# Two chunks of the attention in float32 corners of the array

## The chip, the cores and the metric

The kernel runs on one core of one Trainium2 chip. The metric is the time of one execution on the device in microseconds (us). In the names of the profile, PE is TensorE (matrix products), PEld its weight loads, DVE VectorE, ACT ScalarE, POOL GpSimd and SP SyncE, which issues all DMA transfers here. A program that fixes one order of the instructions on each engine stands behind both kernels; the engines wait for each other by semaphores.

## The reference

A linear attention with a decaying state feeds a feed-forward layer (FFN) with a maximum over three branches.

```python
batch, n_heads, seq, head_dim = (4, 8, 768, 48)
...
for t in range(S):
    kt, vt, rt = (k[:, :, t], v[:, :, t], r[:, :, t])
    cur = np.einsum('bhd,bhe->bhde', u[None] * kt, vt)
    y[:, :, t] = np.einsum('bhd,bhde->bhe', rt, state + cur)
    state = w[None, :, :, None] * state + np.einsum('bhd,bhe->bhde', kt, vt)
...
h = np.maximum(np.maximum(x @ w1, x @ w2), x @ w3)     # x: 3072 x 384, w1 to w3: 384 x 768
return (h @ w_out).astype(np.float32)                  # w_out: 768 x 384, weights in float64
```

## The kernel before

The sequence is cut into 12 chunks of 64 steps (C = 64). A chunk has two halves q of 4 heads, and a half is 8 units (2 pairs of heads by 4 batches). A unit holds two heads: one in partitions 0 to 63, the other in 64 to 127. For each half the attention needs these products, all of them on PE into tiles of the PSUM pool `psa` (4 buffers), and these are the words used below:

- **scores** (sc): the decayed keys kT against the decayed r, 64 by 64 for each head; masked on DVE (`mask`) into the tile am.
- **bonus** (bo): the diagonal of am, from the product pp = kT * rT (`joined`) and a fixed operand spots; DVE lays it on the diagonal (`on_diagonal`).
- **keys turned** (th): the keys transposed against an identity; needed for the state.
- **keys** (ke): the turned keys against v, which are added to the state (`into_state`).
- **values** (va): v against am and the state against r; ACT and DVE take them out as x in two float16 parts, xh and xl (`x_high`, `x_low`).

The FFN of a chunk multiplies x (256 columns, the 64 steps of 4 batches) by 18 weight blocks of three products of three terms each (`up`, hi*hi + hi*lo + lo*hi in float16), takes maxima and multiplies by the third matrix (`down`); these products go into `psm` (4 buffers).

Chunks 1 to 11 work in float16 parts as well: ACT makes the high part of kT, r, am, v, the turned keys and the state, DVE the low part, and a pair of DMAs (`spread`) lays both into a block-diagonal tile, in which the two heads of a unit are one 128 by 128 operand: kd into kb (scores, keys turned), ktd into ktb (keys), vd into vb and sd into sb (values). Chunk 0 is computed in float32: ACT lays kT into the blocks kb and kbx, v into vb and the turned keys into ktb and ktbx (`apart`), and `full` multiplies by operands of 128, 96 or 112 columns. Chunks 0 to 2 (c < EARLY) take their bonus from pp; from chunk 3 on POOL scales k and r and computes the bonus.

The weights come as 16 halves of blocks (words of float64, 576 KB each) into 4 buffers `raw64`; each half takes an ACT cast (`tops`), a DVE `convert`, an ACT `round_up` and a DVE `leave` to become two float16 parts (w_97 to w_104, the last two for `down`). The buffer is free when `leave` is done.

The order of all this is worked out before the program is written: every step is announced with a due time, an engine and a cost (`plan.do`), the table SHIFT adds a correction to the due time for each kind and stage of the program, and `Plan.order` runs a list of ready steps by due time. At the start `stir` runs 20 products of zeros on PE.

## Time and profile before

| | |
|---|---|
| median of 3 runs | 407.06 us (404.7 to 408.22) |
| the profiled execution | 404.66 us |
| its span, first to last instruction | 402.9 us |
| PE busy | 382.0 us (95% of the span) |
| DVE, ACT, POOL busy | 286.8, 264.2, 185.3 us |
| mean granted clock of TensorE | 0.973 of full speed |

The profiled execution is one run with the profiler on; what lies between its span and its time (1.76 us) is start and end outside the core's instructions. Busy times overlap across engines. The granted clock is one number for a stretch of time: 1.00 is 2.4 GHz, 0.50 is 1.2 GHz.

### The profile page before, as it was taken

To read this page: it belongs to the slowest core of one execution; us is meant where nothing else is said; L and a number is where in the kernel's file an instruction comes from. 1 tells how busy PE (TensorE), PEld (TensorE's weight loads), DVE (VectorE), ACT (ScalarE), POOL (GpSimd) and SP (SyncE) were. 2 spreads that over 40 slices of the span, in tenths; PEclk is the share of its full clock that TensorE was granted. 3 is DMA by queue.
4 is the path that set the end of the run, shared out by engine and by line. 5 is a ranking of instruction groups with operands and counts; after the bars stand their busy time and mean duration, and the time that the engine had idled before them with its cause. 6 is when DMAs were issued, how large, how long until landed. Compare 5 with 4: busy or idle time off the path is not lost.

```text
span 402.9 us, 12298 instructions
## 1 busy us (share of the span) xinstructions
PE 382.0 (95%) x4898; PEld 342.4 (85%) x4898; DVE 286.8 (71%) x540; ACT 264.2 (66%) x699; POOL 185.3 (46%) x188
## 2 busy tenths in 40 slices
PE   8699979989999899999999999999999999999994
PEld 4599869879898788999999989988898998999883
DVE  6675999975988978826957948948858875634520
ACT  6865978676776676554764854865775976984421
POOL 9330110184698766415475466465576463120110
PEclk9856999999999999999999999999999999999999
DMA  7877899999969997838678678698599686820101
GB/s 237 306 239 214 247 259 291 250 243 265 253 186 255 248 257 206 211 93 242 188 224 245 181 201 255 173 275 236 136 286 265 160 250 178 219 65 2 39 2 48
DMA packets 29809, 81.89 MB, mean 203 GB/s; under 512 B 4656, under 2 KB 10288, under 8 KB 29744
## 3 DMA queue, kind: packets, MB, share of 16 engines
q1 hardware_dynamic: 29744, 81.03, 72.9%
q8 instruction: 40, 0.66, 0.7%
q14 instruction: 25, 0.20, 0.2%
HBM read 37.59 MB, written 4.72 MB: 105 GB/s over the span
## 4 chain that ended last, share of the span: by engine, by line
PE 63%; DMA 15%; DVE 7%; ACT 6%; issue 5%; SPq 2%; POOL 2%; DVEq 0%; ACTq 0%; POOLq 0%
PE psm L660 48%; PE psa L573 10%; DMA kb<-kd 6%; DMA raw<-in_wo_dram 3%; DMA ktb<-ktd 3%; PE psa L655 2%; DMA tok<-in_tok_dram 2%; PE psa L557 2%; DVE m L679 1%; DMA u_sb<-in_ut_dram 1%; ACT junk L481 1%; POOL feat L499 1%; ACT xh L638 1%; DVE xl L643 1%; DVE sd L628 1%
## 5 line engine op out<-in xcount | busy, mean ns | idle before, releaser
L660 PEld LDWEIGHTS <-w 128*128 128x128 f16 x2592 | 249.3, 98 | 33.3 <-issue 5.0
L660 PE MATMUL psm<-xh,w 128*128 128x256 f16 x1296 | 222.0, 273 | 3.0 <-DVE m L679 1.6
L660 PE MATMUL psm<-xl,w 128*128 128x256 f16 x648 | 153.3, 273 | 0.3 <-DVE xl L643 0.2
L679 DVE SCALAR_TENSOR_TENSOR m<-psm,m 128x256 f32<-128x256 f32 x144 | 60.1, 419 | 38.7 <-PE psm L660 23.0
L688 POOL TENSOR_TENSOR hl<-m,hh 128x256 f16<-128x256 f32 x55 | 39.3, 720 | 89.5 <-ACT hh L682 89.5
L660 PE MATMUL psm<-hh,w 128*128 128x256 f16 x432 | 56.1, 272 | 0.0
L682 ACT CAST hh<-m 128x256 f16<-128x256 f32 x72 | 28.1, 401 | 40.5 <-DVE m L679 40.0
L499 POOL TENSOR_TENSOR feat<-feat,wrt 128x512 f32<-128x512 f32 x36 | 48.3, 1353 | 10.1 <-DMA feat<-in_feat_dram 9.0
L481 ACT ACTIVATE junk<-tok 128x384 bf16<-128x384 f32 x72 | 37.4, 519 | 15.5 <-DMA tok<-in_tok_dram 14.5
L643 DVE SCALAR_TENSOR_TENSOR xl<-psa,xh 32x256 f16<-32x256 f32 (+2 forms) x60 | 28.3, 471 | 13.8 <-ACT xh L638 12.8
L534 POOL TENSOR_TENSOR pp<-feat 128x512 f32<-128x512 f32 x4 | 7.6, 1911 | 57.5 <-DVE feat L499 47.9
L675 ACT ACTIVATE m<-psm 128x256 f32<-128x256 f32 x72 | 27.0, 375 | 10.5 <-PE psm L660 6.7
L660 PE MATMUL psm<-hl,w 128*128 128x256 f16 x216 | 33.4, 273 | 0.0
L573 PE MATMUL psa<-ah,vb 128*128 128x64 f16 x352 | 32.9, 193 | 0.0
L573 PE MATMUL psa<-rh,sb 128*128 128x64 f16 x352 | 32.5, 193 | 0.4 <-DMA sb<-sd 0.2
L573 PE MATMUL psa<-al,vb 128*128 128x64 f16 x176 | 31.2, 193 | 0.7 <-DVE al L593 0.7
L573 PE MATMUL psa<-rl,sb 128*128 128x64 f16 x176 | 31.2, 193 | 0.0
L573 PEld LDWEIGHTS <-vb 128*128 128x128 f16 x528 | 29.0, 98 | 1.7 <-issue 0.9
L628 DVE SCALAR_TENSOR_TENSOR sd<-state,wc,sd 128x192 f16<-128x192 f32 x44 | 29.5, 710 | 0.0
L518 POOL TENSOR_TENSOR am<-tok,u_sb 128x384 f32<-128x384 f32 x18 | 19.8, 1099 | 20.8 <-DVE al L593 15.9
L573 PEld LDWEIGHTS <-sb 128*128 128x128 f16 x528 | 27.5, 98 | 0.6 <-DMA sb<-sd 0.3
L638 ACT ACTIVATE xh<-psa 32x256 f16<-32x256 f32 (+2 forms) x60 | 24.9, 415 | 4.6 <-PE psa L573 3.0
(116 smaller groups left out, 609.6 us busy)
## 6 DMA issues: line engine op xcount, KB each, us to landing
tok<-in_tok_dram SPq DMA_DIRECT2D x24, 576.0 KB, 6.7
feat<-in_feat_dram SPq DMA_DIRECT2D x22, 512.0 KB, 4.5
raw<-in_ws_dram SPq DMA_DIRECT2D x12, 576.0 KB, 6.1
kb<-kd SPq DMA_DIRECT2D x22, 256.0 KB, 5.2
kb<-kd SPq DMA_DIRECT2D x22, 248.0 KB, 5.8
ktb<-ktd SPq DMA_DIRECT2D x20, 256.0 KB, 5.3
ktb<-ktd SPq DMA_DIRECT2D x20, 248.0 KB, 5.5
out_dram<-io SPq DMA_DIRECT2D x36, 128.0 KB, 2.6
```

The costliest lines, as they stand in the source:

```text
L481: nc.scalar.activation(out=junk[:, 0:U * D].rearrange("p (u d) -> p u d", u=U), in_=src, func=AF.Square, scale=scale, accum_out=stat[:, ki ...
L499: helper(c).tensor_tensor(out=t[n], in0=t[n], in1=tb, op=ALU.mult)
L518: helper(c).tensor_tensor(out=w.rearrange("p (g b) d -> p g b d", g=2), in0=t["r"], in1=by_token(u_sb, q), op=ALU.mult)
L573: nc.tensor.matmul(out=ps, lhsT=l[i], rhs=rr[j], start=first and n == 0, stop=last and n == 2)
L628: nc.vector.scalar_tensor_tensor(out=sd[q].dense[:, 1, us, 0:D], in0=state[:, j], scalar=wc[:, j:j + 1], in1=sd[q].dense[:, 0, us, 0:D], o ...
L638: nc.scalar.mul(out=hi, in_=src, mul=SC_X)
L643: nc.vector.scalar_tensor_tensor(out=lo, in0=src, scalar=SC_X, in1=hi, op0=ALU.mult, op1=ALU.subtract)
L660: nc.tensor.matmul(out=ps, lhsT=a, rhs=b, start=first and n == 0, stop=last and n == len(prods) - 1)
L675: nc.scalar.mul(out=m, in_=ps, mul=by)
L679: nc.vector.scalar_tensor_tensor(out=m, in0=ps, scalar=by, in1=m, op0=ALU.mult, op1=ALU.max)
L682: nc.scalar.copy(out=h[0][:, f, :], in_=m)
L688: lows_by(c, f).tensor_tensor(out=h[1][:, f, :], in0=m, in1=h[0][:, f, :], op=ALU.subtract)
```

## The change

Chunk 1 is computed in float32 too (FULL = 2), and both chunks in another form. Scores, keys turned and keys take kT, rT, the turned keys (a plain tile kt) and v as they lie in memory, without block-diagonal operands: each head of a unit is one product of 64 by 64 (48 columns for the keys), whose operands lie in partitions 0 to 63 or 64 to 127 and whose result goes to the same partitions of PSUM (`corners`). 16 such products replace 8 of 128 columns in chunk 0, and 24, 16 and 24 float16 products in chunk 1. Only the values still need block-diagonal operands: v is loaded by DMA straight into its places in vb (`load_values`, pieces of 48 floats), and for chunk 1 POOL lays the decayed state into sb (`state_apart`). With this go, for chunk 1, the float16 parts of kT, r, am, v and the turned keys and the spreads into kb, ktb and vb, and for the state after chunk 0 its parts and the spread into sb; for chunk 0 the `apart` copies on ACT.

POOL instead of DVE now scales kT and rT of chunks 1 and 2. The clearing of kb moves from DVE and shrinks. `stir` is announced six more times with two products of 512 columns each, due last (FILLS). A path that would compute xl by products (`x_taken_off`) is there, but with APART = 0 no chunk takes it; its two tiles minus and moved are filled all the same, on POOL. The clock model of the planner and the whole table SHIFT are new, so the order of steps changes on every engine through the whole program. Chunks 2 to 11 and the FFN keep their arithmetic.

```diff
-EARLY = 3
+FULL, EARLY, APART = 2, 3, 0
+FILLS = 6
...
-    STAGES = (1.6, 4.2)
+    RATE = {"feat": 330e3, "tok": 330e3, "word": 330e3, "again": 330e3, "u": 330e3, "vl": 200e3, "kb": 215e3, "ktb": 240e3, "sb": 240e3, "vb": 220e3, "io": 300e3}
+    STAGES = (-0.01, 1.6, 4.2)
...
-        "act ah": (9.25, -3.6, 2.69),
-        "act hh": (-13.49, -31.97, -10.54),
...
+        "act ah": (3.099, -10.12, -11.987, -18.156),
+        "act hh": (33.605, 41.616, -9.662, 26.229),
...
+    def load_values(c, q, hh):
+        w = vb[q].wide[HS[hh], :, hh * D:(hh + 1) * D].rearrange("p (g b) d -> p g b d", g=2)
+        nc.sync.dma_start(out=w, in_=tok[c, q][HS[hh], 2])
...
-    kb = Block("kb", P, nc.vector)
-    kbx = Block("kbx", P)
+    vb = [Block(f"vb{q}", 2 * D) for q in range(2)]
     amt = [const.tile([P, U, C], F32, name=f"am{q}") for q in range(2)]
-    nc.gpsimd.memset(amt[0], 0.0)
-    vb = [Block("vb0", 2 * D)]
-    nc.gpsimd.memset(amt[1], 0.0)
-    vb.append(Block("vb1", 2 * D))
+    for t in amt:
+        nc.gpsimd.memset(t, 0.0)
     for z in ztop:
         nc.gpsimd.memset(z.bitcast(F32), 0.0)
-    ktb = Block("ktb", P)
-    ktbx = Block("ktbx", P)
+    if FULL > 1:
+        sb = [Block(f"sb{q}", 2 * D) for q in range(2)]
+    moved = const.tile([P, 2, NJ, P], F16, name="moved")
+    nc.gpsimd.memset(moved.bitcast(F32), 0.0)
     kd = Block("kd", P)
+    kb = Block("kb", P, edge=C)
     vd = [Block(f"vd{q}", 2 * D) for q in range(2)]
+    ktd = Block("ktd", P)
+    ktb = Block("ktb", P, edge=C)
...
-        helper(c).tensor_tensor(out=t[n], in0=t[n], in1=tb, op=ALU.mult)
+        (nc.gpsimd if c else nc.vector).tensor_tensor(out=t[n], in0=t[n], in1=tb, op=ALU.mult)
...
+    def corners(ps, n, l, r):
+        for i in range(U):
+            for hh in range(2):
+                nc.tensor.matmul(out=ps[HS[hh], i, 0:n], lhsT=l(i, hh), rhs=r(i, hh), start=True, stop=True)
+
     def keys_turned(c, q):
         t = raws[c, q]
-        if c == 0:
-            t["th"] = psa.tile([P, U, D], F32, name="psa")
-            for i in range(U):
-                nc.tensor.matmul(out=t["th"][:, i, :], lhsT=(kb, kbx)[q].wide[:, i, :], rhs=eye[:, 0:D], start=True, stop=True)
+        if c < FULL:
+            t["th"] = psa.tile([P, U, C], F32, name="psa")
+            k = units(t["kT"])
+            corners(t["th"], C, lambda i, hh: k[HS[hh], i, :], lambda i, hh: eye[HS[hh]])
...
+            t["kt"] = work.tile([P, U, C], F32, name="kt")
+            nc.scalar.copy(out=t["kt"], in_=t.pop("th"))
+            return
...
+            k, r = units(t["kT"]), units(t["rT"])
+            corners(t["sc"], C, lambda i, hh: k[HS[hh], i, :], lambda i, hh: r[HS[hh], i, :])
...
+            corners(t["ke"], D, lambda i, hh: t["kt"][HS[hh], i, :], lambda i, hh: vb[q].wide[HS[hh], i, hh * D:(hh + 1) * D])
...
+        joint = c < APART
+        for i in range(U):
+            if c < FULL:
+                n = R
+                prods = [(vb[q].wide[:, i, 0:R], t["a"][:, i, :])]
+                if c:
+                    prods.append((sb[q].wide[:, i, 0:R], units(t["rT"])[:, i, :]))
...
+    def state_apart(q):
+        for hh in range(2):
+            w = sb[q].wide[HS[hh], :, hh * D:(hh + 1) * D].rearrange("p (g b) d -> p g b d", g=2)
+            by = wc[HS[hh], 2 * q:2 * q + 2].unsqueeze(2).unsqueeze(3).broadcast_to([C, 2, B, D])
+            nc.gpsimd.tensor_tensor(out=w, in0=state[HS[hh], 2 * q:2 * q + 2], in1=by, op=ALU.mult)
...
+    def values_fetched(c, q, due):
+        for hh in range(2):
+            dma(due + 0.01 * hh, lambda hh=hh: load_values(c, q, hh), 98304, writes=[("vb", q), ("vl", q)], kind="vl")
...
+    def entire(c, q, due):
+        f, v = ("feat", c, q), ("vb", q)
+        k, r, last = ("kT", c, q), ("rT", c, q), c + 1 == FULL
         scaled(c, q, due)
-        do(due - 0.29, "act", 1.05, lambda: apart((kb, kbx)[q], units(raws[c, q]["kT"]), C), reads=[("kT", c, q)], writes=[b], kind="kba")
-        do(due - 0.10, "act", 0.85, lambda: apart(vb[q], units(raws[c, q]["v"]), D, SC_V), reads=[t], writes=[("vb", q)], kind="vba")
+        do(due, "pe", 1.3, lambda: scores(c, q), reads=[f, k, r], takes=[("psa", ("sc", c, q))], active=0.66, kind="sca")
         before_mask(c, q, due)
-        do(due, "pe", 1.75, lambda: full("sc", q, (kb, kbx)[q], C, P, units(raws[c, q]["rT"])), reads=[f, b, ("rT", c, q)], takes=[("psa", ("sc", c, q))], active=0.5, kind="sca")
         do(due + 0.02, "dve", dve(U * C), lambda: mask(c, q), reads=[("sc", c, q)], writes=[("am", c, q)])
-
-    def first_values(q, due):
-        c = 0
-        do(due, "pe", 1.32, lambda: full("va", q, vb[q], C, R, raws[c, q]["a"]), reads=[("am", c, q), ("vb", q)], takes=[("psa", ("va", c, q))], active=0.66, kind="vaa")
-        leave_x(c, q, due)
-
-    def first_keys(q, due):
-        c, t, b, k = 0, ("tok", 0, q), ("kb", "kbx")[q], ("ktb", "ktbx")[q]
-        do(due - 0.30, "pe", 1.75, lambda: keys_turned(c, q), reads=[b], takes=[("psa", ("th", c, q))], active=0.4, kind="tha")
-        do(due - 0.24, "act", 0.85, lambda: apart((ktb, ktbx)[q], raws[c, q].pop("th"), C), reads=[("th", c, q)], writes=[k], kind="ktba")
-        do(due, "pe", 1.55, lambda: full("ke", q, (ktb, ktbx)[q], D, C + D, units(raws[c, q]["v"])), reads=[k, t], takes=[("psa", ("ke", c, q))], active=0.43, kind="kea")
-        after_keys(c, q, due)
+        do(due + 0.1, "pe", 1.29 * (2 if c else 1), lambda: values(c, q), reads=[("am", c, q), v] + ([f, r, ("sb", q)] if c else []), takes=[("psa", ("va", c, q))], active=0.66, kind="vaa")
+        leave_x(c, q, due + 0.1)
+        do(due + 0.2, "pe", 1.3, lambda: keys_turned(c, q), reads=[f, k], takes=[("psa", ("th", c, q))], active=0.66, kind="tha")
+        do(due + 0.22, "act", act(U * C), lambda: keys_laid(c, q, 0), reads=[("th", c, q)], takes=[("kt", ("kt", c, q))])
+        do(due + 0.3, "pe", 1.2, lambda: keys(c, q), reads=[("kt", c, q), v], takes=[("psa", ("ke", c, q))], active=0.55, kind="kea")
+        after_keys(c, q, due + 0.3)
...
+        if c + 1 < FULL:
+            do(due + 0.06, "pool", 2.0, lambda: state_apart(q), reads=[s], writes=[("sb", q)], near=0.55)
+            return
...
+    for k in range(FILLS):
+        do(90, "pe", 0.43, lambda: stir(2, 2 * TOK), reads=["stirred"] if k else [], writes=["stirred"], takes=[("psm", ("fill", k))], kind="fill")
+    attend(0, -0.8)
```

The names in the orders that follow: psa and psm are the PSUM pools; feat holds kT and rT, cs the identity, tok the values and vb, am, spots and pp are as above. First PE, from the end of the 20 stir products to the first float16 product, before:

```order
L412 MATMUL psa<-cs,tkf 128x128 x4
L655 MATMUL psa<-feat,kb 128x64 x8
L544 MATMUL psa<-pp,spots 128x256 x2
L655 MATMUL psa<-feat,kbx 128x64 x8
L544 MATMUL psa<-pp,spots 128x256 x2
L655 MATMUL psa<-am_161,vb_164 96x64 x8
L557 MATMUL psa<-cs,kb 128x48 x8
L655 MATMUL psa<-am_162,vb_167 96x64 x8
L544 MATMUL psa<-pp,spots 128x256 x2
L655 MATMUL psa<-tok,ktb 112x48 x8
L557 MATMUL psa<-cs,kbx 128x48 x8
```

Each batch of 8 here is one half's product, in operands of 96 to 128 columns. The same place on PE now, to the second values product:

```order
L573 MATMUL psa<-cs,feat 64x64 x16
L573 MATMUL psa<-feat 64x64 x16
L562 MATMUL psa<-pp,spots 128x256 x2
L573 MATMUL psa<-vb_160,kt 64x48 x16
L562 MATMUL psa<-pp,spots 128x256 x2
L662 MATMUL psa<-am_164,vb_160 96x64 x8
L573 MATMUL psa<-cs,feat 64x64 x16
L573 MATMUL psa<-feat 64x64 x16
L429 MATMUL psa<-cs,tkf 128x128 x4
L573 MATMUL psa<-vb_162,kt 64x48 x16
L662 MATMUL psa<-am_165,vb_162 96x64 x8
```

Scores, keys turned and keys have become batches of 16 corners, and the keys now stand here for both halves. From there to the FFN's first products:

```order
L382 LDWEIGHTS still
L382 MATMUL psm<-still 128x512
L382 LDWEIGHTS still
L382 MATMUL psm<-still 128x512
L573 MATMUL psa<-cs,feat 64x64 x16
L573 MATMUL psa<-feat 64x64 x16
L562 MATMUL psa<-pp,spots 128x256 x2
L573 MATMUL psa<-vb_160,kt 64x48 x16
L716 LDWEIGHTS w_97
```

Chunk 0 has its keys ahead of its values, all float32 work of chunk 0 stands ahead of the FFN, and so do keys turned, scores, bonus and keys of chunk 1's first half. After these follow 18 FFN products, the values of chunk 1's first half, the bonus and scores of its second half, 45 FFN products, its values, and the rest of chunk 1 between FFN products. Before, the keys of the second half of chunk 0 and all of chunk 1 but keys turned and scores of one half stood behind the FFN's first product.

SP, which issues the transfers in this order, from the load of chunk 1's first half on, before (L281 loads kT and rT, L292 v, L330 weights, L442 and L443 spread):

```order
L281 DMA feat<-in_feat_dram 128x1024
L292 DMA tok<-in_tok_dram 128x384
L281 DMA feat<-in_feat_dram 128x1024
L330 DMA raw_286<-in_ws_dram 128x2304
L330 DMA raw_303<-in_ws_dram 128x2304
L442 DMA kb<-kd 64x2048
L443 DMA kb<-kd 64x1984
L330 DMA raw_345<-in_ws_dram 128x2304
L330 DMA raw_362<-in_ws_dram 128x2304
L292 DMA tok<-in_tok_dram 128x384
L281 DMA feat<-in_feat_dram 128x1024
L442 DMA vb_164<-vd_177 64x1536
```

Between the weights stand a spread into kb and one into vb. The same now (L287 and L298 are these loads, L340 weights):

```order
L287 DMA feat<-in_feat_dram 128x1024
L298 DMA vb_160<-in_tok_dram 64x8x48 x2
L340 DMA raw_356<-in_ws_dram 128x2304
L287 DMA feat<-in_feat_dram 128x1024
L340 DMA raw_404<-in_ws_dram 128x2304
L298 DMA vb_162<-in_tok_dram 64x8x48 x2
L340 DMA raw_436<-in_ws_dram 128x2304
L340 DMA raw_492<-in_ws_dram 128x2304
L340 DMA raw_546<-in_ws_dram 128x2304
L287 DMA feat<-in_feat_dram 128x1024
L302 DMA tok<-in_tok_dram 128x384
L340 DMA raw_577<-in_ws_dram 128x2304
```

The spreads of chunk 1 are gone from between the weights; loads of v in pieces stand there instead.

POOL, after it has cleared the tiles, now (before, the first of these places held four pp products and nothing else until chunk 3's scaling):

```order
L418 ISA
L418 TENSOR_SCALAR minus<-cs 128x128
L420 TENSOR_SCALAR moved<-cs 32x32 x3
L418 TENSOR_SCALAR minus<-cs 128x128
L420 TENSOR_SCALAR moved<-cs 32x32 x3
L668 TENSOR_TENSOR sb_170<-state,wc 64x8x48 x2
L517 TENSOR_TENSOR feat<-feat,wrt 128x512 x2
L552 TENSOR_TENSOR pp<-feat 128x512
L668 TENSOR_TENSOR sb_172<-state,wc 64x8x48 x2
```

The scaling of chunk 1 now stands on POOL behind the unused minus and moved and behind the first half's state.

## Rows read from the trace of the kernel before

**Rows 1.** The page: the span, and the granted clock in 40 slices of it.

```profile
span 402.9 us, 12298 instructions
...
PEclk9856999999999999999999999999999999999999
```

**Rows 2.** Windows: stretch, length, busy of PE, PEld, DVE, ACT, POOL, PEclk, DMA share, GB/s.

```profile
9.00:12.80 3.80, 3.80 (x31) 3.56 (x30) 0.48 (x1) 3.67 (x9) 3.80 (x6) 1.00 1.03 421
12.80:15.60 2.80, 0.01 (x1) 0.03 (x1) 1.78 (x4) 2.77 (x5) 0.91 (x2) 1.00 1.00 401
...
16.00:16.50 0.50, 0.50 (x3) 0.40 (x2) 0.50 (x2) 0.50 (x1) 0.00 (x0) 0.62 0.06 22
...
20.00:34.00 14.00, 14.00 (x69) 13.61 (x69) 10.21 (x17) 9.09 (x18) 3.54 (x1) 0.50 0.74 231
34.00:36.40 2.40, 2.40 (x45) 2.34 (x45) 0.00 (x0) 0.48 (x1) 0.00 (x0) 0.50 1.00 270
...
36.60:38.00 1.40, 1.40 (x14) 1.26 (x13) 1.40 (x3) 0.43 (x2) 0.00 (x0) 1.00 0.87 273
36.20:396.80 360.60, 350.06 (x4714) 315.91 (x4711) 263.47 (x494) 239.38 (x652) 168.60 (x164) 1.00 0.74 201
40.00:80.00 40.00, 36.71 (x490) 32.55 (x488) 39.61 (x77) 32.46 (x73) 4.11 (x3) 1.00 0.99 261
```

**Rows 3.** Chain that ended last, 10 to 40 us: start, length, what.

```profile
17.52 2.79 PE psa L655 x16
20.32 3.39 PE psa L557 x16
23.70 2.59 PE psa L655 x16
```

**Rows 4.** Timeline of PE, 7 to 47 us: start, length, what, idle before.

```profile
7.78 0.60 PE L412 MATMUL psa<-cs,tkf 128*128 128x128 f32 x4
8.21 1.94 PE L655 MATMUL psa<-feat,kb 128*128 128x64 f32 x16
9.99 1.08 PE L544 MATMUL psa<-pp,spots 128*128 128x256 f32 x4
10.91 1.90 PE L655 MATMUL psa<-feat,kbx 128*128 128x64 f32 x16
15.61 1.55 PE L544 MATMUL psa<-pp,spots 128*128 128x256 f32 x4 [2.80 <-DVE pp L534]
...
36.20 0.40 PE L660 MATMUL psm<-xh,w 128*128 128x256 f16 x1
...
45.23 1.68 PE L655 MATMUL psa<-tok,ktbx 128*112 128x48 f32 x16
46.75 0.27 PE L660 MATMUL psm<-xh,w 128*128 128x256 f16 x1
```

**Rows 5.** Chain that ended last, 84 to 122 us: float16 products of a half.

```profile
90.50 0.40 PE psa L562 x16
90.89 0.70 PE psa L573 x24
95.53 1.41 PE psa L573 x48
...
117.39 0.60 PE psa L573 x24
```

**Rows 6.** Groups by line and shape on DVE, 0 to 80 us: busy, mean ns.

```profile
L499 DVE TENSOR_TENSOR feat<-feat,wrt 128x512 f32<-128x512 f32 x12 | 7.9, 683 | 0.3 <-DMA feat<-in_feat_dram 0.3
...
L628 DVE SCALAR_TENSOR_TENSOR sd<-state,wc,sd 128x192 f16<-128x192 f32 x8 | 4.0, 543 | 0.0
```

**Rows 7.** Timeline of POOL, 14 to 100 us.

```profile
22.51 3.54 POOL L534 TENSOR_TENSOR pp<-feat 128x512 f32<-128x512 f32 x1 [8.79 <-DVE feat L499]
...
57.29 1.26 POOL L534 TENSOR_TENSOR pp<-feat 128x512 f32<-128x512 f32 x1 [9.63 <-DMA sb<-sd]
...
80.91 2.52 POOL L499 TENSOR_TENSOR feat<-feat,wrt 128x512 f32<-128x512 f32 x2 [2.07 <-DMA feat<-in_feat_dram]
```

**Rows 8.** Timeline of all engines, 395 us to the end.

```profile
396.66 0.19 PE L736 MATMUL psa<-good,ones 128*1 128x1 f32 x2
396.77 0.38 ACT L705 ACTIVATE io<-psm 128x256 f32<-128x256 f32 x1 [1.58 <-PE psm L660]
```

**Rows 9.** The page, DMA issues: queue, count, KB each, us to landing.

```profile
out_dram<-io SPq DMA_DIRECT2D x36, 128.0 KB, 2.6
```

More of the change, by code (lines that the diff above doesn't have):

```diff
@@ L181, in order @@
     def order(self):
-        free, pipe, clock = dict(self.FREE), 0.0, Clock(-0.3)
+        free, pipe, clock = dict(self.FREE), 0.0, Clock(-0.3, self.FREE["pe"])
         left, gone, landed = {}, {}, []
@@ L403, with subtrahends @@
     turned = []
+    minus = const.tile([P, 2, P], F16, name="minus")
+    def subtrahends():
+        for z, by in enumerate((SC_X * SC_V, SC_X)):
+            nc.gpsimd.tensor_scalar(out=minus[:, z], in0=ident, scalar1=-1.0 / by, scalar2=None, op0=ALU.mult)
+            for j in range(NJ):
+                nc.gpsimd.tensor_scalar(out=moved[R:P, z, j, 32 * j:32 * (j + 1)], in0=ident[R:P, R:P], scalar1=-1.0 / by, scalar2=None, op0=ALU.mult)
     def twice():
@@ L472 @@
     state = const.tile([P, NP, B, D], F32, name="state")
-    nc.gpsimd.memset(state, 0.0)
     stat = const.tile([P, 4, 2 * NCH], F32, name="stat")
@@ L602, in into_state @@
         ps = raws[c, q].pop("ke")
+        if c == 0:
+            nc.scalar.copy(out=units(state[:, 2 * q:2 * q + 2]), in_=ps)
+            return
+        by = wcv if c == FULL else wc
         for g in range(2):
@@ L998, in leave_x, with x_lo_act @@
         left = dict(takes=[("xl", lo)]) if q == 0 else dict(writes=[lo])
-        do(due + 0.04, "dve", 0.62 if q == 0 else 1.7, x_lo, reads=[("va", c, q), hi], **left)
+        if c >= APART:
+            do(due + 0.04, "dve", 0.62 if q == 0 else 1.7, x_lo, reads=[("va", c, q), hi], **left)
+            return
+        def x_lo_act():
+            if q == 0:
+                T["x", c][1] = xp.tile([P, NJ, TOK], F16, name="xl")
+            x_rest(c, q, T["x", c][1])
+        do(due + 0.035, "pe", 0.22 if q == 0 else 0.44, lambda: x_taken_off(c, q, T["x", c][0]), reads=[hi, "minus"], writes=[("va", c, q)], kind="xs")
+        do(due + 0.04, "act", 0.6 if q == 0 else 1.55, x_lo_act, reads=[("va", c, q)], **left)
     def attend(c, at):
@@ L1005, in attend @@
             due = at + 0.5 * q
+            if c < FULL:
+                entire(c, q, due)
+                continue
             scaled(c, q, due + 0.05)
@@ L1015, in attend @@
                 keyed(c, q, due + 0.12)
-                spread_state(c, q, due + 0.32)
     parts = ((0,), (0, 1), (1,))
@@ L1080 @@
             weight(n, h, 0.11 * n + 0.05 * h - 0.4)
-    for q in range(2):
-        first_keys(q, 0.1 + 0.2 * q)
-        spread_state(0, q, 0.2 + 0.2 * q)
     for c in range(NCH):
```

261 lines of the change are left out of this document (139 added, 122 removed).

## The prediction

> **What bounds the kernel now.** I read the page's line of clock slices first, then windows of all engines around its dip, then the chain and PE's timeline inside it, and last the end. The clock stands at half only in slices 2 to 4 of 40 [rows 1]; elsewhere PE is simply full. The windows date the dip: PE works until 12.8 us, does nothing for 2.8 us, and in the stretch 16.0 to 16.5 the mean clock is 0.62, so it fell at 16.1 (0.12 us at full, the rest at half). From 20 to 34 PE is busy without a gap and still at 0.50; after 34.0, when float16 products run, it returns by 36.6 [rows 2]. So 20 us of dense PE work ran at 1.2 GHz, which costs 10 us, and all of it lies on the chain [rows 3]. The gap comes from the second bonus, which waits for pp on DVE [rows 4]; DVE there stood behind weight conversions, whose ACT casts stood behind the copies of v.
>
> The first FFN product starts at 36.2 [rows 4]. From there to the last product PE is busy 350.1 of 360.6 us [rows 2], so whatever advances the FFN's start and adds no PE work behind it shortens the run one for one. Between 40 and 80 us DVE is busy 39.6 of 40 us and DMA 0.99 [rows 2]: an earlier FFN gains only if these two come earlier as well.
>
> **The change part by part.** *Price of a corner.* The float32 products come as two passes each in the trace. Start to start, a pass with 128 stationary columns takes (9.99 - 8.21) / 16 = 111 ns, with 112 columns (46.75 - 45.23) / 16 = 95 ns [rows 4], with 96 columns 2.59 / 16 = 162 ns at half clock, 81 at full [rows 3]. That is 0.85 ns per stationary column, whatever streams past (64 or 48). No corner is in the trace. One after the other, a corner of 64 columns costs 2 x 54 ns and a batch of 16 takes 1.74 us; if the two corners of a unit overlap fully, 0.87. I take 1.3 (keys 1.2): the middle, and the price in the diff's plan, whose prices for the old batches (1.75, 1.75, 1.55, 1.32) meet the rows (16 x 0.111 = 1.78, 3.39 / 2 = 1.70, 1.52, 2.59 / 2 = 1.30) [rows 3, 4]. Both ends stay in the range.
>
> A rule speaks for the upper end. The Trainium skill, "PSUM — Partial Sum Buffer", section "PSUM bank collisions raise a hardware error", quotes that different row tiles cannot access one PSUM bank at the same time, and both corners of a unit write the same bank. By that rule the two run one after the other and the batch takes 1.74; the result below would be 5 us later, still faster than before. No run here shows it yet.
>
> *PE up to the FFN.* The 20 stir products end at 7.9 as before, since turn starts at 7.8 [rows 4]. Then nine corner batches (six of 1.3, three of 1.2) = 11.4; three bonuses of 0.46 (two took 10.91 - 9.99) [rows 4]; two values products of 1.30 [rows 3]; turn 0.43 [rows 4]; two stir products of 512 columns, at twice the 0.11 of 256 columns, 0.44 [rows 2]; 0.4 for small waits. Sum 16.7, the FFN starts at 24.5 instead of 36.2. This holds at full clock, so the waits in it matter. kT and rT no longer pass through ACT: kT is scaled by about 6.5, and the first keys turned can follow stir at once. Behind each wait PE has other work: keys turned and scores of a half need only DVE's 0.68 us scalings [rows 6], the ACT copy of the turned keys runs beside scores and bonus, mask (two DVE passes after the bonus) beside keys and the next bonus. DVE does pp and both masks of half 0 ahead of the first weight conversion, so the 2.8 us gap has no successor there. What can be late next is POOL: chunk 1's first load was in by 16.0, when the DMA share drops to 0.06 [rows 2]; I allow 17. Its three steps of 1.26 us (kT, rT, pp) [rows 7] end at 20.8, PE wants kT at 20.2 (it has been ready since 18.3), pp at 22.8: cover of 2 us. POOL's first arithmetic took 3.54 us once [rows 7]; it now falls on the unused minus, in front of the state and of these scalings, and ends at about 15. If POOL were later by more than 2 us, PE waits that much.
>
> *PE behind the FFN's start.* Left there before: one keys (1.52) [rows 4], one bonus (0.46), and of chunk 1 in float16 keys turned 0.40, scores 0.70, two values of 1.41, two keys of 0.60 [rows 5] = 7.1. Left there now: two values of chunk 1 with 16 products each (2 x 2.60), bonus 0.46, scores 1.3, keys turned 1.3, keys 1.2 = 9.5. So 2.4 more.
>
> *DVE, ACT and DMA* hide the earlier FFN, if they shrink by as much as it advances, 11.7. DVE loses 14 passes over 512 columns (kT and rT scalings of chunks 1 and 2, low parts of kT, r, am) of 0.68 us, two low parts of v (0.5 each) and four state passes of 0.54 [rows 6]: 12.7. DMA loses eight spreads, 2 x (0.52 + 0.52 + 0.39 + 0.39) MB = 3.6 MB, at the 261 GB/s of that stretch [rows 2] 13.9 us; the loads of v are the same bytes in 192-byte pieces, bounded by nothing extra and by twice their time (0.8 MB, 3 us). ACT loses about as many passes as DVE. So the three keep pace, with little to spare on DVE, and I leave PE's idle time from the FFN on at its old 10.5 us; the new due times may make it 5 or 14.
>
> *The end.* Five pairs of stir products are left over behind the last product and the count, 2.2 us on PE. The last output leaves ACT at 397.15 and takes 2.6 us plus issue to land, past 399.9 [rows 8, 9], while PE would be done at 399.0, so I count nothing and keep 2.2 as the upper bound.
>
> **Sum.** 24.5 + 350.1 + 2.4 + 10.5 + 6.1 (from 396.8 to the end) = 393.6, against a span of 402.9: 9.3 less. The profiled execution's own time was 404.66, so 395.4. The median before is 2.4 above that execution; part of its spread should be the place where the clock falls, which goes away, so I take 397.0 as the median now.
>
> **The rivals.** *The clock falls all the same.* For it: float32 work did not raise the clock in 14 dense us [rows 2], so one gap early in a longer float32 stretch is paid to its end; and a corner uses a quarter of the array. Against: dense float32 work from 9.0 to 12.8 held 1.00 [rows 2], and PE has no gap of more than 0.5 us in my account. If it falls at 16, 8.4 us of work left before the FFN double, and 1 to 2 us are lost until float16 raises it: 405 (range 402 to 409). The Trainium skill, "TensorE: Matmul & The Clock Gate", Part 1, has activity release the throttle and idleness bring it back, and says nothing of float32; the dense 14 us at half clock differ from its plain form.
>
> *A corner costs as much as a whole pass* (slower). If each pass takes 111 ns whatever its columns, since two small tiles alternate and neither load hides, a batch is 3.55, twelve batches add 27 us, and the time is 422. It decides from 2.1 us per batch (9.3 us over 12), 65 ns per pass; the columns' slope, 111, 95, 81, leads to 54 and speaks against it.
>
> *The FFN catches up with its weights.* Nothing is wrong before 24.5, but conversions on DVE and ACT, paced by four buffers, or the spread for chunk 2's scores (now behind all the weights on SP) come later than PE. The lead of 11.7 against DVE's 12.7 makes a few us likely, all 9 unlikely: 400 to 405. That the change does not do what it says, the two corners of a unit running one after the other, is the upper end of the first sum, 402.
>
> **How the numbers follow.** Forecast, clock held and corners between 0.87 and 1.74: 0.68. Clock falls: 0.15. Corners dear: 0.07. FFN waits: 0.10. About 1% (4 us) is what a measurement of this kernel can tell from no change. Forecast's own range: the POOL chain forbids more than 1.5 us below the FFN's start, corners behind it 1.3, idle 5.5 less, giving 390 against the 397; serial corners 5, idle 3.5 more, not all at once, 403. Of the clock's and the waits' cases most lies under 406. Range 390 to 406. Faster by over 1% (under 403): nearly all of the forecast, a third of the waits, a little of the clock: 0.72. Slower by over 1% (over 411): dear corners and the worst of the clock: 0.10. Within 1%: 0.18.
>
> **What would show it.** Right: granted clock 1.00 in all slices after the first two, first FFN product at 23 to 28, a corner batch of 0.9 to 1.75 start to start, no chunk 1 work from ACT's and DVE's float16 parts, PE idle 5 to 14 us from then to the last product. Wrong: clock 0.50 past 16 us, a corner batch over 2.1, or waits of PE for weights, kb or DVE that add up to more than 9 us between 25 and 80.

## The result and the profile after

The changed kernel takes 390.31 us (388.19 to 395.22, 4 runs) beside 407.64 (404.7 to 410.8) for the kernel before in the same session: a ratio of 0.958, 95% interval 0.950 to 0.966. The ratio leaves out the run of 395.22, which counts as slow because it is over 1.5% above the fastest. The forecast was 397.0 in a range of 390 to 406. The profiled execution took 388.19 us, its span is 386.3, against 404.66 and 402.9 before; on both sides it is the fastest of the four.

The page answers to [rows 1]: no slice shows a lower clock.

```profile
span 386.3 us, 12522 instructions
...
PEclk9999999999999999999999999999999999999999
```

PE's timeline from 7 to 27 us answers to [rows 3, 4]: start, length, tile, pass count, and the idle time before it.

```profile
8.09 1.15 PE L573 MATMUL psa<-cs,feat 64*64 64x64 f32 x32
9.07 1.10 PE L573 MATMUL psa<-feat 64*64 64x64 f32 x32
10.10 1.13 PE L562 MATMUL psa<-pp,spots 128*128 128x256 f32 x4
11.16 1.13 PE L573 MATMUL psa<-vb,kt 64*64 64x48 f32 x32
12.22 1.13 PE L562 MATMUL psa<-pp,spots 128*128 128x256 f32 x4
13.19 1.49 PE L662 MATMUL psa<-am,vb 128*96 128x64 f32 x16
...
19.77 0.59 PE L382 MATMUL psm<-still 128*128 128x512 f16 x2
20.55 1.15 PE L573 MATMUL psa<-cs,feat 64*64 64x64 f32 x32 [0.18 <-POOL feat L517]
22.29 1.15 PE L573 MATMUL psa<-feat 64*64 64x64 f32 x32 [0.59 <-POOL feat L517]
24.04 1.13 PE L562 MATMUL psa<-pp,spots 128*128 128x256 f32 x4 [0.60 <-POOL pp L552]
25.10 1.14 PE L573 MATMUL psa<-vb,kt 64*64 64x48 f32 x32
26.16 0.28 PE L716 MATMUL psm<-xh,w 128*128 128x256 f16 x1
```

Read the starts, not the lengths, since neighbours overlap: a corner batch (16 products, 32 passes) takes 9.07 - 8.09 = 0.98, 10.10 - 9.07 = 1.03 or 12.22 - 11.16 = 1.06 us. The first FFN product starts at 26.16 instead of 36.20.

The chain from 8 to 30 us shows what the last 6 us of that hang on; the last line is from POOL's timeline and holds the two scalings together.

```profile
10.21 8.57 DMA feat<-in_feat_dram
...
20.46 1.78 POOL feat L517
22.24 0.07 issue
22.31 1.67 POOL pp L552
```

```profile
18.95 3.29 POOL L517 TENSOR_TENSOR feat<-feat,wrt 128x512 f32<-128x512 f32 x2 [0.87 <-DMA feat<-in_feat_dram]
```

Chunk 1's feature load is issued at 10.21, behind four weights, and lands at 18.79; then POOL scales twice (18.95 to 20.46 and 1.78 from there) and multiplies (1.67): 1.5 to 1.8 us a step where [rows 7] had 1.26.

Windows (columns as in [rows 2]) from the FFN's start to the last product, and of the two stretches behind 40 us:

```profile
26.10:379.90 353.80, 349.36 (x4675) 317.47 (x4671) 251.97 (x483) 237.52 (x635) 176.58 (x170) 1.00 0.72 200
40.00:80.00 40.00, 37.73 (x449) 33.66 (x450) 34.03 (x60) 26.94 (x63) 15.32 (x14) 1.00 0.70 214
80.00:380.00 300.00, 299.61 (x4092) 273.38 (x4090) 204.04 (x405) 200.68 (x554) 151.99 (x151) 1.00 0.72 196
```

PE is busy 349.36 of 353.8 us, so it idles 4.4 where it idled 10.5 [rows 2]. DVE and DMA, full between 40 and 80 us before [rows 2], have slack now, and from 80 to 380 PE idles 0.4 us. In the kernel before that last window is:

```profile
80.00:380.00 300.00, 292.75 (x4042) 265.21 (x4039) 216.42 (x404) 200.32 (x563) 161.82 (x157) 1.00 0.75 203
```

7.25 us idle. The end, answering to [rows 8]:

```profile
379.89 0.19 PE L792 MATMUL psa<-good,ones 128*1 128x1 f32 x2
380.02 2.33 PE L382 MATMUL psm<-still 128*128 128x512 f16 x10
```

So the span's 16.6 us divide into 10.0 for the FFN's earlier start (36.2 to 26.2), 0.7 for PE's busy time behind it (350.06 to 349.36), 6.1 for its idle time there (10.54 to 4.44), less 0.2 at the end (6.2 to 6.4 from the count's product on).

The 10.0 us can be taken apart too, from the first batch on (8.21 and 8.09). Before, PE worked 5.1 us at full and 19.7 us at half clock, which is 15.0 us of work at full clock, and waited 3.2 (2.80 and 0.37). Now it works 16.7 and waits 1.4. So there is 1.7 us more work ahead of the FFN, since that of chunk 1's first half now stands there, and 1.8 us less waiting; what is left, some 10 us, is the clock.

### The profile page after: what moved, and what is told of

The parts are those of the page before. It is cut to its first block, busy times and chain, and to the rows that moved or that the text cites. A ratio compares the mean times of both kernels' runs of the same rounds, so it can differ in the third digit from the quotient of the medians.

```text
span 386.3 us, 12522 instructions
## 1 busy us (share of the span) xinstructions
PE 375.4 (97%) x5038; PEld 335.4 (87%) x5038; DVE 272.7 (71%) x520; ACT 254.8 (66%) x669; POOL 200.1 (52%) x207
## 2 busy tenths in 40 slices
DMA packets 32177, 78.29 MB, mean 203 GB/s; under 512 B 8560, under 2 KB 13680, under 8 KB 32112
## 4 chain that ended last, share of the span: by engine, by line
PE 78%; ACT 6%; DMA 6%; POOL 3%; DVE 2%; issue 2%; SPq 0%; DVEq 0%; POOLq 0%; ACTq 0%
PE psm L716 61%; PE psa L662 7%; PE psa L601 5%; PE psm L382 2%; ACT junk L369 2%; DMA feat<-in_feat_dram 2%; DMA vb<-vd 2%; DMA tok<-in_tok_dram 2%; POOL feat L517 1%; PE psa L573 1%; ACT junk L502 1%; POOL pp L552 1%; DVE hl L744 1%; PE psa L562 1%; POOL sb L668 1%
## 5 line engine op out<-in xcount | busy, mean ns | idle before, releaser
L716 PE MATMUL psm<-xh,w 128*128 128x256 f16 x1296 | 219.8, 273 | 1.9 <-DVE m L735 1.9
L517 POOL TENSOR_TENSOR feat<-feat,wrt 128x512 f32<-128x512 f32 x44 | 59.8, 1376 | 36.5 <-DMA feat<-in_feat_dram 36.4
L699 DVE SCALAR_TENSOR_TENSOR xl<-psa,xh 32x256 f16<-32x256 f32 (+2 forms) x60 | 28.3, 471 | 10.5 <-ACT xh L694 8.9
L662 PE MATMUL psa<-ah,vb 128*128 128x64 f16 x320 | 29.5, 193 | 0.4 <-DMA vb<-vd 0.4
L662 PE MATMUL psa<-rh,sb 128*128 128x64 f16 x320 | 29.5, 193 | 0.0
L662 PE MATMUL psa<-rl,sb 128*128 128x64 f16 x160 | 28.4, 193 | 0.0
L662 PE MATMUL psa<-al,vb 128*128 128x64 f16 x160 | 28.4, 193 | 0.0
L662 PEld LDWEIGHTS <-vb 128*128 128x128 f16 x480 | 25.7, 98 | 0.9 <-issue 0.6
L662 PEld LDWEIGHTS <-sb 128*128 128x128 f16 x480 | 25.0, 98 | 0.0
L545 POOL TENSOR_TENSOR am<-cs,a 128x512 f32<-128x512 f32 x18 | 19.9, 1107 | 8.8 <-DVE a L541 8.5
L681 DVE SCALAR_TENSOR_TENSOR sd<-state,wc,sd 128x192 f16<-128x192 f32 x36 | 22.2, 656 | 1.4 <-ACT sd L674 1.4
```

Of the source, the lines that this page charges most:

```text
L517: (nc.gpsimd if c else nc.vector).tensor_tensor(out=t[n], in0=t[n], in1=tb, op=ALU.mult)
L545: helper(c).tensor_tensor(out=t["a"], in0=eye.unsqueeze(1).broadcast_to([P, U, C]), in1=t.pop("sum").unsqueeze(2).broadcast_to([P, U, C]), ...
L662: nc.tensor.matmul(out=t["va"][0:n, i, :], lhsT=a, rhs=b, start=k == 0 and (i == 0 or not joint), stop=k == len(prods) - 1, skip_group_che ...
L681: nc.vector.scalar_tensor_tensor(out=sd[q].dense[:, 1, us, 0:D], in0=state[:, j], scalar=by[:, j:j + 1], in1=sd[q].dense[:, 0, us, 0:D], o ...
L699: nc.vector.scalar_tensor_tensor(out=lo, in0=src, scalar=x_scale(c), in1=hi, op0=ALU.mult, op1=ALU.subtract)
L716: nc.tensor.matmul(out=ps, lhsT=a, rhs=b, start=first and n == 0, stop=last and n == len(prods) - 1)
```

## Experiments

The theory after the result (A in most runs) had three parts: the new start, in corners, holds the clock and brings the FFN forward; the rest of the gain is idle time behind the start; and that time goes because the new due times fit the new program. The rivals: the old gap alone had cost the clock; the late due times are simply better, or do nothing and the lighter DVE and DMA load does it all; chunk 1's form rather than chunk 0's carries the gain. The runs were made four at a time on one chip, and ratios are to the kernel before in the same four: 404.9 us (the filled gap, the cold start, the corners in series, the old late due times), 407.5 (the new due times in the kernel before, chunk 0 alone, the early load, a control) and 405.0 (the last four).

### Was it the gap that cost the clock?

Thirteen idle products in the 2.8 us gap of the kernel before:

```diff
         t["bo"] = psa.tile([P, U, C], F32, name="psa")
+        if c == 0 and q == 1:
+            stir(13, 2 * TOK)
```

> The kernel before, with 13 products of zeros on TensorE in its 2.8 us gap at 12.8 us, so that the clock should stay at 1.00 through the float32 stretch; all else is as before, the due times too. If the half clock alone cost the 10 us (my theory for the start), the first FFN product comes at 26 to 27 us instead of 36.2 and the time falls by 8 to 10, to 398 to 400. If the relief of DVE and DMA by chunk 1 in float32 was needed as well (first rival), the FFN starts early but waits for weights and DVE behind it, and the time is 402 to 407. If float32 does not hold the clock even without a gap, the granted clock falls all the same and nothing changes.

Measured: 408.83 us, ratio 1.012 (1.008 to 1.016). PE's timeline of this run, and its windows (length, PE busy, granted clock, DMA share, GB/s):

```profile
17.96 1.54 PE L657 MATMUL psa<-am,vb 128*96 128x64 f32 x16 [0.82 <-ACT w L351]
19.34 1.94 PE L559 MATMUL psa<-cs,kb 128*128 128x48 f32 x16
22.39 1.83 PE L657 MATMUL psa<-am,vb 128*96 128x64 f32 x10 [1.11 <-DVE am L585]
```

```profile
21.00:22.00 1.00, 0.28 (x3) 1.00 1.00 290
22.00:23.00 1.00, 0.61 (x4) 0.50 0.87 217
```

The clock outlived the filled gap and fell at 22 us all the same, at a wait of 1.1 us behind 128-column float32 products; the FFN started at 36.62. This is the third of the expected outcomes, the clock that falls all the same, and the time is 1.2% longer. So that one gap was not the whole cause. The old start had the next waits ready: 0.82 us at 17.1, and 1.11 at 21.3.

### Do the corners raise the clock, or only keep it?

The changed kernel with 3 idle products ahead of the start in place of 20:

```diff
-    stir(20, 2 * TOK)
+    stir(3, 2 * TOK)
```

> The changed kernel with 3 instead of 20 products of zeros at the start, so that PE stands idle from about 2.4 to 6.5 us and begins its float32 stretch at half clock. If float32 work, corners included, does not raise the clock (my rival in the prediction), it stays at 0.50 until float16 products run behind 26 us, batches take 2.0 us, the FFN starts at 38 to 41 and the time is 400 to 405. If dense corners do raise it, the clock is back by 12 to 16 us and the time is 391 to 395.

Measured: 393.71 us, ratio 0.972 (0.966 to 0.979).

```profile
6.70 1.97 PE L573 MATMUL psa<-cs,feat 64*64 64x64 f32 x32 [4.14 <-DVE feat L517]
8.46 1.92 PE L573 MATMUL psa<-feat 64*64 64x64 f32 x32
10.30 2.07 PE L562 MATMUL psa<-pp,spots 128*128 128x256 f32 x4
12.31 1.30 PE L573 MATMUL psa<-vb,kt 64*64 64x48 f32 x32
13.54 1.13 PE L562 MATMUL psa<-pp,spots 128*128 128x256 f32 x4
14.51 1.49 PE L662 MATMUL psa<-am,vb 128*96 128x64 f32 x16
...
26.25 0.28 PE L716 MATMUL psm<-xh,w 128*128 128x256 f16 x1
```

The first two batches and the bonus take 1.8 to 2.0 us, twice their time; from 12.3 on the same products take 1.23 and 0.97, close to the 1.06 and 0.97 of the changed kernel. Nothing but float32 had run on PE since 6.7. The FFN starts at 26.25, as late as with a warm start, since it waits for POOL. So float32 work raises the clock as well, here two batches of corners and one bonus of 128 columns; which of the two did it, this run does not tell apart. The time lies in the expected 391 to 395, but the loss of 2 to 5 us against the runs of the changed kernel is not at the FFN's start: in the profile PE idles 8.4 us between there and the last product, where it idled 4.4. What the cold start changes there was not tried.

### Do the two corners of a unit overlap?

All upper corners of a batch ahead of all lower ones, in place of upper and lower by turns:

```diff
-        for i in range(U):
-            for hh in range(2):
+        for hh in range(2):
+            for i in range(U):
```

> The changed kernel, with the eight corners of the lower partitions first and the eight of the upper ones after them in each batch, so that neighbours share rows and columns of the array. If the 1.0 us of a batch rests on two corners overlapping in different rows (theory), a batch takes 1.7 us as the slope of 0.85 ns per column and pass says, 12 batches cost 8 us more PE work and the time is 395 to 399, since nine of them stand on the path ahead of the FFN, partly beside POOL's waits. If a pass of 64 columns simply takes 32 ns (rival), batch and time stay.

Measured: 392.48 us, ratio 0.969 (0.962 to 0.976), span 390.8. The first batch of keys turned:

```profile
8.42 1.72 PE L573 MATMUL psa<-cs,feat 64*64 64x64 f32 x29
9.93 0.27 PE L573 MATMUL psa<-feat 64*64 64x64 f32 x1
...
11.75 1.13 PE L562 MATMUL psa<-pp,spots 128*128 128x256 f32 x4
...
30.86 0.28 PE L716 MATMUL psm<-xh,w 128*128 128x256 f16 x1
```

The two batches up to the bonus take 11.75 - 8.42 = 3.33, or 1.67 each and 52 ns a pass; by turns they took 2.01. So neighbours in different rows overlap for most of their time, close to the 0.87 of full overlap and far from 1.74; whether their products overlap or only a weight load and a product, the times do not tell. The Trainium skill, "PSUM — Partial Sum Buffer", section "PSUM bank collisions raise a hardware error", quotes two statements: different row tiles cannot access one bank at the same time, different column tiles can, on separate partitions. The prediction named the first alone and read it as corners that take turns, which that section of the Trainium skill does not say; the corners of a unit lie in different row tiles and different column tiles, and in this trace 0.98 to 1.06 a batch stands against the 1.74 of turns. For these pairs the times go with the second.

The batch is as expected, the time is not: 395 to 399 was forecast. The FFN started at 30.86, 4.7 us later than in the changed kernel, and the span is 4.5 longer. That is not one for one: from the FFN's start to the last product there are 1.7 us more PE work, for the three batches that stand there, and 2.0 less idle time. The later FFN waited less.

### What are the due times worth?

The changed kernel with the last two columns of its table taken from the old one (chunks 2 and on; a name that the old table lacks keeps its new value), and the kernel before with its late columns from the new one:

```diff
-        "act ah": (3.099, -10.12, -11.987, -18.156),
+        "act ah": (3.099, -10.12, -3.6, 2.69),
...
```

> The changed kernel with the corrections to the due times of its last two stages (due after 1.6, so all from the FFN of chunk 2 on) taken from the table of before, where that table has the step; its first two stages and all arithmetic stay. If the new due times are what took PE's waits behind 80 us from 7.3 to 0.4 us (theory), 5 to 8 us come back and the time is 395 to 399. If the waits went because DMA and DVE have less to do and the FFN runs ahead (rival), the time stays at 389 to 392.

> The kernel before (float16 chunks 0 and 1, old start) with its due times from the third stage on (due above 1.6, which is chunk 2 and later) taken from the changed kernel's table; where a name has no entry there, the old value stays. Theory A, a due-time table fits only the program that it was found for (the order, the costs and the buffers of that program): the kernel before gains nothing, 402 to 420 us, TensorE still idle for 7 us or more behind 80 us. Theory B, the new table is better for the late chunks of any such program, and this is where 7 us of the gain came from: 396 to 400 us, with less than 2 us of idle behind 80 us.

Measured: 402.33 us, ratio 0.989 (0.979 to 0.9998), and 418.73 us, ratio 1.030 (1.021 to 1.039). The window from 80 us on, and what PE waits for there (us, times, longest), of the changed kernel with the old late columns:

```profile
80.00:380.00 300.00, 293.66 (x4008) 265.06 (x4006) 211.32 (x402) 199.28 (x556) 153.40 (x152) 1.00 0.72 197
```

```profile
PE psa L601 <- DMA ktb<-ktd: 3.3, 3, 2.0
PE psa L601 <- DMA kb<-kd: 1.1, 1, 1.1
```

The same window of the kernel before with the new ones:

```profile
80.00:380.00 300.00, 287.65 (x3963) 259.74 (x3960) 193.53 (x382) 196.50 (x548) 159.56 (x155) 0.99 0.75 201
```

Idle from 80 to 380 us: 7.25 before, 0.4 after, 6.3 with the old late columns, 12.4 in the kernel before with the new ones. With the old columns the FFN starts at 26.79, DVE and DMA have no less slack between 40 and 80 us, and most of the gain is gone. Of both expectations the side holds that a table serves the program that it was found for, and the lighter load by itself did not bring the idle time down. But 402.33 lies above the 395 to 399 expected there. The profile shows two causes more, a wait of 3.1 us for POOL at 65 us and the clock at half behind it; the rest of the 12 us above the changed kernel was not taken apart. One rival is left: both runs join columns of two tables, and no run has a table found anew for the kernel before. How far such a search alone would bring its 7.25 us down, and so how much of the 6.1 us the change itself is worth, stays open.

### Chunk 0 alone in corners

```diff
-FULL, EARLY, APART = 2, 3, 0
+FULL, EARLY, APART = 1, 3, 0
```

> The changed kernel with chunk 0 alone in float32 corners and chunk 1 by the float16 products again (its SC_V scaling, spreads and splits are back for chunk 1; the due times stay). The plan puts ten idle products between chunk 0's attention and the first FFN product. Theory A, chunk 0's corners alone keep the clock and make the early start, chunk 1's float32 form is worth its removed splits and spreads only: granted clock 0.99 or more all through, first FFN product at 21 to 24 us, but idle time of 4 to 10 us between 24 and 80 us while chunk 1's split, spread and pair products find DVE and the DMA queues full of weights: 391 to 400 us. Theory B, chunk 1's float32 form is what holds the gain: the FFN is as late as in the kernel before (34 us or later) or the clock falls to half in the gap, 402 to 412 us.

Measured: 405.25 us, ratio 0.997 (0.993 to 1.002). The FFN starts at 21.53, and then PE waits; the first FFN product, the waits of 20 to 80 us, and two windows of three in which the clock falls:

```profile
21.53 0.27 PE L716 MATMUL psm<-xh,w 128*128 128x256 f16 x1
...
PE psm L716 <- DVE w L365: 6.3, 4, 2.8
PE psm L716 <- ACT w L361: 5.6, 3, 3.4
```

```profile
30.00:34.00 4.00, 2.53 (x12) 0.61 0.72 192
...
60.00:68.00 8.00, 4.77 (x58) 0.60 0.73 211
```

The time is B's, the mechanism is neither's: the start is early, as A had it, the clock falls not in the old gap but in float16 work that waits for converted weights. With FFN products 5 us sooner, and chunk 1's splits back on DVE and ACT, the weights are not there. How much of the 15 us is the table, which was not found for this program, stays open.

### The first load of chunk 1

The fourth weight's load behind chunk 1's first feature load in place of ahead of it, and POOL's diagonals and copies, which nothing reads, left out:

```diff
+        feat = [i for i, p in enumerate(out) if p["kind"] == "sp feat"][4]
+        word = max(i for i, p in enumerate(out[:feat]) if p["kind"] == "sp word")
+        out.insert(feat, out.pop(word))
...
-    do(-0.72, "pool", 1.6, subtrahends, writes=["minus"], kind="minus")
+    do(-0.72, "pool", 1.6, lambda: None, writes=["minus"], kind="minus")
```

> The changed kernel with chunk 1's first feature load issued ahead of the fourth weight load (it is behind it in the changed kernel) and without POOL's two diagonals and six 32 by 32 copies at 11.4 to 15.9 us, which nothing reads. Theory A, the FFN's start hangs on this load and then on POOL (feat issued 10.2, landed 18.8, POOL's scalings and products 18.95 to 23.9): the load lands at 16.5 to 17.5, the first FFN product starts at 24.3 to 25.2 instead of 26.2, and 0.5 to 1.8 us of it reach the end: 387 to 390 us, ratio to the changed kernel 0.995 to 0.999. Theory B, the fourth weight, which now lands later, is what the first FFN products wait for, or the time won is given back as idle time between 26 and 60 us: the same time within 0.3% or up to 1 us slower.

With it, on the same chip, the changed kernel unaltered:

> The changed kernel once more, unaltered, as the control of the three runs beside it. Both theories: 388 to 392 us, as measured the first time; a median outside of it would show how far runs of one session stand from those of another.

Measured: 392.86 us, ratio 0.962 (0.953 to 0.971), beside 391.66, ratio 0.960 (0.949 to 0.970), for the control. PE's timeline with the early load, and its windows:

```profile
24.36 0.28 PE L720 MATMUL psm<-xh,w 128*128 128x256 f16 x1
...
28.73 0.38 PE L666 MATMUL psa<-am,vb 128*96 128x64 f32 x2 [1.80 <-DVE am L619]
```

```profile
28.00:30.00 2.00, 1.27 (x15) 1.00 0.59 240
30.00:32.00 2.00, 2.00 (x16) 0.51 0.15 30
```

A's first half holds: POOL starts at 16.95, the FFN at 24.36. The second does not: the 1.8 us come back as a wait for DVE's mask at 26.9, and behind it the clock falls, from 30 until 37 us. B is right. The length of that wait alone does not make the clock fall: the profile of the cold start has one of 2.3 us, for the same mask and ahead of the same products (28.4 to 30.7 us), and behind it the clock stays at 1.00.

### Where the changed kernel's own spread is from

Its two profiles so far differ most in one wait, PE's for POOL's product of chunk 2 ahead of that chunk's second bonus. Six idle products in that wait; four, and the product on DVE; and the control:

```diff
         t = raws[c, q]
+        if (c, q) == (2, 1):
+            stir(6, 2 * TOK)
...
-        joins(c).tensor_tensor(out=t["pp"], ...
+        (nc.vector if c == 0 or (c, q) in [(2, 1)] else nc.gpsimd).tensor_tensor(out=t["pp"], ...
```

> The changed kernel unaltered, the control of the three beside it: 388 to 393 us. Its two profiles so far differ at one place, ahead of chunk 2's second bonus products: 1.9 us of waits between 60 and 75 us and the clock at full in the run of 388.2 us, one wait of 2.7 us for POOL's product and the clock at half from about 67.5 to 71 us in the run of 391. Theory A, that wait decides the kernel's spread: the profiled run shows either the short wait with full clock and 390 us or less, or the long wait with a stretch at half clock and 391 us or more. Theory B, the spread has nothing to do with it: a long wait with a fast run, or the reverse.

> The changed kernel with six idle products (1.3 us at full clock) ahead of chunk 2's second bonus products, in the wait for POOL. Theory A, TensorE's idle time there lets the clock fall and the half clock behind it costs 1.7 us a time: the clock stays at 1.00 from 60 to 80 us, and the runs lie at 387 to 391 us, with the upper ones of the control gone; where the wait is short the products cost up to 0.9 us. Theory B, the wait alone is the cost and the dip is only seen beside it: the dip stays or goes, the median is the control's within 0.2% or 1 us slower.

> As the one before with four idle products (0.9 us), and chunk 2's second kT times rT product on DVE in place of POOL, at the place in the program where POOL had it. Theory A, POOL is what the wait ends on (POOL's 1.4 to 1.8 us behind its scalings become DVE's 0.7 us): the wait ahead of these bonus products shrinks by about 1 us, and the median by 0.5 to 1.5 us against the changed kernel. Theory B, DVE comes to the product later than POOL does (it stands behind the value split, which took until 64.1 and 65.7 us in the two profiles, and holds up the float16 conversions behind it): no gain or up to 1 us slower.

Measured: control 388.71 us, ratio 0.963 (0.958 to 0.968); filled 390.18, ratio 0.967 (0.962 to 0.973); filled and on DVE 390.48, ratio 0.966 (0.962 to 0.971). The wait in PE's timeline, and the windows around it, in the first control (profiled run 391.19 us):

```profile
67.00 1.56 PE L562 MATMUL psa<-pp,spots 128*128 128x256 f32 x4 [2.69 <-POOL pp L552]
```

```profile
66.00:68.00 2.00, 1.00 (x4) 0.89 0.43 130
68.00:70.00 2.00, 2.00 (x28) 0.50 0.00 0
70.00:72.00 2.00, 2.00 (x16) 0.76 0.00 0
```

POOL's scalings for it start when the load lands, at 62.39 here, at 60.30 and 61.16 in the two profiles without a dip:

| profiled run | time, us | PE's waits there, us | clock 66 to 72 us |
| --- | --- | --- | --- |
| changed kernel, first | 388.19 | none for POOL, 1.9 for DVE | 1.00 |
| changed kernel, third | 388.84 | none for POOL, 1.5 for DVE | 1.00 |
| changed kernel, second | 391.19 | 2.7 for POOL | half from 67.6 to 71.0 |
| with one pair of end products | 392.11 | 2.6 for POOL, 0.2 for ACT | half from 66.8 to 70.2 |

The stretch at half clock costs 1.7 us (half of what lies between 67.6 and 71.0), the longer wait about 1. A is borne out by these four profiles, which are few, and only in part by the runs without one: a run of this control took 392.16 us at a mean clock of 0.998, by which the clock cost it about 0.8 us. So the dip is one source of the spread and not the only one. The remedies failed. Filled, the clock stays at 1.00 from start to end in the profiled run, but the idle products take a result buffer and wait 1.9 us for ACT to clear it:

```profile
66.94 1.46 PE L382 MATMUL psm<-still 128*128 128x512 f16 x6 [1.90 <-ACT m L733]
```

The upper runs that were to go are still there: three of the other five have a mean clock of 0.989 to 0.997, the slowest 393.73 us. On DVE the product comes at 67.97, later than POOL's end at 64.4 in the first profile, and the clock falls elsewhere, from 41.4 to 48.2 us. Neither beats the control, so no version here beats the changed kernel.

### The products at the end

```diff
-FILLS = 6
+FILLS = 1
```

> The changed kernel with one pair of idle products at the very end instead of six. Theory A, the ten that go lie behind the last FFN product and beside the last eviction and the last transfer, so that they cost nothing: the same time within 0.3%, and from the last FFN product's end to the span's end 6.0 to 6.4 us as before. Theory B, they are on the path to the end or delay the branch behind them: 1 to 2.2 us faster.

Measured: 392.86 us (390.23 to 396.2), ratio 0.970 (0.962 to 0.977). From the count, at 382.60, to the span's end, 388.9, it is 6.3 us, against 6.4 with six pairs: within the span the products at the end cost nothing. The time is 4 us above the control's, where the same within 0.3% was expected. Its profile has the wait and the dip of the table. Another 1.4 us lie outside the span: a run's time is 3.2 to 3.3 us longer than its span in all four runs here, and 1.7 to 1.9 in all runs of the changed kernel. What stands there, and why it grows when the end products go, no run shows.

## Why the prediction came out as it did

**The clock: right, for a reason only half seen.** 1.00 in every slice. The forecast put the dip down to one gap; filling it did not save the old start. The new start, corners with short waits (0.18, 0.59, 0.60 us), did hold the clock, and a cold start showed that such work raises it too. That rules out what the first rival had argued from, that float32 does not raise it: the 14 us of [rows 2] were 128-, 112- and 96-column products. The Trainium skill, "TensorE: Matmul & The Clock Gate", Part 1, has activity release the throttle; with the corners the trace of the cold start agrees (products at half speed to 12.3 us, close to full from there). Whether it is the shape or the shorter waits that tell the two forms apart was not tried.

**The FFN's start: 24.5 forecast, 26.16 measured, with two errors that nearly cancel.** Taken from 8.09 us on, the 16.7 us became 18.1. The corner batch was mis-sized from above: 1.3 (keys 1.2), measured 0.98 to 1.06 where PE does not wait; nine of them take 9.5 in place of 11.4. The bonus was misread: the "x4" of the row at 9.99 in [rows 4] is one bonus of two products in two passes each, not two bonuses, so three of them take 3.1 in place of 1.4. Values, turn and idle products are 0.6 above. The waits were 1.4 in place of 0.4: the load that was to land by 17 landed at 18.79, POOL's steps took 1.5 to 1.8 in place of 1.26, so kT was ready at about 20.5 and the product at 24.0 in place of 18.3 and 20.8. The "cover of 2 us" was the right thing to compute, and used up. Of the 10.0 us gained here nearly all is the clock, as the prediction's 10 us at half clock said; what the corners saved was taken up by work of chunk 1.

**PE behind the start: 352.5 forecast, 349.4 measured.** Three cheaper corner batches (1.07 to 1.08 each) are 0.6 of it; 2.2 lie in the FFN's group of xh products (222.0 to 219.8 us by the trace's modelled ends for the same 1296), and what they are was not tried.

**Idle time behind the start: the term that failed.** It was kept at its old 10.5 because DVE, ACT and DMA would lose as much work as the FFN came forward. Mostly they lost it (78.29 MB moved where 81.89 had been, the 3.6 MB of the forecast; DVE's busy time went from 286.8 to 272.7 us, ACT's only from 264.2 to 254.8), and the lead was kept; but the 4.4 us left lie below the range of 5 to 14 that the forecast gave. The lighter load was not enough to remove the 7.25 us from 80 us on: with the old late columns 6.3 us are idle there, under the new load. The prediction named the new due times in half a sentence, and gave them a range of 5 to 14 with no row to work it out from.

**The end: right**, 6.4 against 6.1, and the products behind the count are hidden within the span.

**The sum.** Against the forecast span of 393.6 the start is 1.7 us late, PE behind it 3.1 less, its idle time 6.1 less and the end 0.3 more, which makes the 386.3 but for rounding. The median, 390.31, lies in the range by 0.3 us, and that is luck: it rests on the late start, which offsets a part of what PE's work and idle time came out lower, and the last control's median, 388.71, lies under 390. The lower bound was itself misadded, since 397.0 less 1.5, 1.3 and 5.5 is 388.7. And the 422 of the dear corners is counted from 395, the other cases from 397.

**The rivals.** Dear corners fell at once. The clock's fall did not come at the start, but stands at 67 us in some runs. The FFN that catches up with its weights did not come either, but is what happens with chunk 0 alone in corners, under due times found for another program: there the weights set the pace. That whatever advances the FFN shortens the run one for one does not hold as it stands: in the profiles 4.7 us later gave back 2.0 us of idle time, and 1.8 us earlier brought nothing where the next producer was already at its limit.

## What to carry to other kernels

When small dense blocks can stand in quarters of the array, price them by stationary columns and let neighbours alternate between row halves; here that made float32 cheap enough to drop a whole chain of splits and copies at the start. Ask which term of the sum an earlier start comes from: here it was the clock, and the cheaper products paid for work moved forward. Look at an order found by search as a part of the program: price it by the idle time of stretches that the edit does not touch, and expect it to be wrong for any other variant, experiments included. And before pulling a start forward, look who is next in line: a wait removed from one product came back whole at the next, and once with a lower clock on top.

## What the runs showed of the hardware

- Float32 passes of 64 by 64 cost 31 to 33 ns each when the two row halves alternate into one result tile, and 52 ns in series; a row from the kernel before had 111 ns for 128 stationary columns.
- In the cold start the granted clock's row reads 1.00 from the beginning while the products run at half speed until 12.3 us (batches of 0.98 and 1.03 us take 1.76 and 1.84): at the start of that trace the row is no evidence, and the duration of a known product is.
- PE's wait of 1.8 us with the early load was followed by half clock from 30 us on, and a wait of 2.3 us at the same place in the cold start's run was not (1.00 from 28 to 40 us).
- A POOL pass over 512 float32 columns took 1.5 to 1.8 us while DVE was 98% busy (20 to 26 us), against 1.26 at 57.29 us in [rows 7]. DVE was busy through the whole of that one too, so its busy time does not tell the two apart; what does stays open.
